# Regrouping score rows by two ten-row transfers with spaced source rows, in a talking-heads attention and gated layer kernel

## The chip, the cores and the metric

The kernel runs on one core of one Trainium2 chip, in one launch. The metric is the device time of that launch in microseconds (us). Times are compared by medians of several runs; the trace that is read here is of one profiled execution. Engines are named as the profile names them: PE (TensorE matmul), PEld (its weight load), DVE (VectorE), ACT (ScalarE), POOL (GpSimd), SP (SyncE, which issues transfers here).

## What is computed

Batch 4, 12 heads, 448 positions, head dimension 64, all in float32. Cut to what matters:

```python
scores = scale * np.matmul(q, k.transpose(0, 1, 3, 2))
scores = np.einsum('bhij,hg->bgij', scores, w_pre)      # first mix over heads
scores = scores - np.max(scores, axis=-1, keepdims=True)
attn = np.exp(scores)
attn = attn / (np.sum(attn, axis=-1, keepdims=True) + 1e-09)
attn = np.einsum('bhij,hg->bgij', attn, w_post)         # second mix over heads
attn_out = np.matmul(attn, v)
x = attn_out.transpose(0, 2, 1, 3).reshape(1792, 768)
gate = 1.0 / (1.0 + np.exp(-(x @ w_gate)))              # 768 x 1536
val = x @ w_val
return gate * val @ w_out                               # 1536 x 768
```

The two mixes contract over heads, so a query row of all 12 heads has to lie on the partitions before it can be mixed by a matmul.

## The kernel before

The attention is cut into 16 blocks: four per batch, of 120, 120, 120 and 88 query rows. Scores of a block are made on PE, two heads at a time (`scores`, L134), and copied to an SBUF tile `st` with query rows on the partitions and, in each partition, 12 heads by 448 keys (`keep`, L143; even pairs of heads on DVE, odd ones on ACT). There are two such tiles, one for even and one for odd blocks.

A block is then worked off in sets of ten rows; two sets make a unit, so a block of 120 rows has six units and one of 88 rows has nine sets (the last begins at row 78 and repeats two rows) and so five units, the last with one set. In all there are 92 units: 88 with two sets and 4 with one. For each unit:

- `regroup` (L169) moves score rows from `st` into a tile `T`, of which there are three. Each transfer takes five neighbouring partitions of `st` (five query rows) and writes 60 partitions of `T` (row by head), 448 floats each. A unit with two sets needs four transfers, all issued by SP: the first set lies on partitions 0 to 59, the second on 64 to 123, and the two halves of a set lie beside each other in the free dimension (index x).
- `premix` (L178) is the first mix: four PE matmuls of 60 rows by 448 columns against the block diagonal weights `w1`, into PSUM banks `pm`. `rowmax` (L186, DVE), `expo` (L194, ACT), `norm` (L202, DVE), `scale` (L207, POOL) and `p_lo` (L223, DVE) make the softmax, split in two float16 parts for most units (`pairs`); the first 6 and the last 8 units stay in float32 and scale the weights instead.
- `postmix` (L231) is the second mix, which also brings keys onto the partitions; `mix` (L243, ACT) copies it from its one PSUM tile into the tile `mixes` of the block. `av` (L251) multiplies by v, copies the result (ACT) and stores it to DRAM from ACT's queue.

The order of work is written out by hand, slot by slot (L345 to L391), one slot per unit. In slot s the program issues, in this order: `regroup(s + 4)`; `premix(s + 2)` and `rowmax(s + 2)`; the scores of the next block that are due; `norm` and `scale` of unit s + 1; `mix(s - 1)`; the copies of those scores; `p_lo(s + 1)`; loads of q, k and v from ACT's queue; `expo(s + 2)`; tasks of the gated layer; `postmix(s)`; and the `av` steps that are due. Every engine runs its own instructions in this order. `regroup(u)` can start when its `T` is free, that is when `premix(u - 3)` is done, and when its block's `st` is complete; the copy of a later block into the same `st` has to wait for the last regroup of the block before the last. The transfers of SP and of ACT take turns on a few completion semaphores, so a transfer is issued only when the one that had its semaphore before has landed.

The gated layer (class `_Moe`, from L414) is a planned list of tasks: its weights are loaded, converted and split in the last units of the attention and behind it, and its matmuls (L818 and L829) fill PE to the end.

Of the kernel before, what the change touches and what calls it, by code (L numbers as in the profile page):

```python
# [22 lines left out]
R = 10  # L23
HALF = 5
# [3 lines left out]

def _blocks(S):
    return [(i0, min(QB, S - i0)) for i0 in range(0, S, QB)]  # L30


def _key_blocks(S):
    return [0, 128, 256, S - 128]


def _attention(ctx, tc, ins, B, H, S, D, xs, raws, make_moe):

    nc = tc.nc
    qp, kp, vb = (ins[n] for n in ("qp", "kp", "vb"))  # L40
# [3 lines left out]
    HK = HALF * H  # L44
# [3 lines left out]
    JB = _key_blocks(S)  # L48
# [18 lines left out]
    PM = 3  # L67
    pm = ps_pm.tile([128, PM, 512], F32, name="pm")

    def two_banks(pool, tag):  # L70
        return pool.tile([128, 2, 512], F32, tag=tag, name=tag)
# [3 lines left out]
    w1 = const.tile([128, 64], F32, name="w1")  # L75
# [24 lines left out]
    blocks, units, NG, ring = [], [], 0, 0  # L100
    for b in range(B):
        for i0, n in _blocks(S):
            rows = [min(r0, n - R) for r0 in range(0, n, R)]
            blocks.append((b, i0, n, len(units)))
            for i in range(0, len(rows), 2):
                r0s = rows[i:i + 2]
                units.append((len(blocks) - 1, r0s, [(ring + k) % PM for k in range(len(r0s))], NG))
                ring += len(r0s)
                NG += len(r0s)
    NU = len(units)  # L110
# [12 lines left out]

    def q_load(bi, eng=None):

        b, i0, n, _ = blocks[bi]
        t = qst.tile([128, NP * QB], F32, tag="q", name="q")
        (eng or nc.scalar).dma_start(out=t[:, :NP * n], in_=qp[b, :, NP * i0:NP * (i0 + n)])
        q_t[bi] = t[:, :NP * n].rearrange("p (c s) -> p c s", s=n)


    st_t = {}

    def scores(bi, c, sc):  # L134
        b, _, n, _ = blocks[bi]
        q, k = q_t[bi], k_t[b, c]
        cuts = [(0, 64), (64, n)] if n > 96 else [(0, n)]
        for s0, s1 in cuts:
            for e in range(2):
                rows = slice(64 * e, 64 * e + 64)  # L140
                nc.tensor.matmul(sc[s0:s1, e, :S], lhsT=q[rows, c, s0:s1], rhs=k[rows, :], start=True, stop=True)  # L141

    def keep(bi, c, sc):  # L143
        n = blocks[bi][2]
        if c == 0:
            st_t[bi] = stg[bi % 2].tile([QB, H, S], F32, tag="st", name="st")
        out, src = st_t[bi][:n, 2 * c:2 * c + 2], sc[:n, :, :S]
        if c % 2:
            nc.scalar.copy(out, src)
        else:  # L150
            nc.vector.tensor_copy(out, src)  # L151
# [10 lines left out]
    t_t, nm_t, e_t, ss_t, p_t, mx_t = {}, {}, {}, {}, {}, {}  # L162
    mixes = [mp.tile([128, 4, H, QB], F32, name=f"mix{i}") for i in range(2)]

    def pairs(u):

        return PB + 2 <= u < NU - 8

    def regroup(u):  # L169
        bi, r0s, _, _ = units[u]  # L170
        T = tp.tile([128, 2, S], F32, tag="T", name="T")
        for i, r0 in enumerate(r0s):
            for x in range(2):
                r = r0 + HALF * x
                nc.sync.dma_start(out=T[64 * i:64 * i + HK, x], in_=st_t[bi][r:r + HALF])  # L175
        t_t[u] = T

    def premix(u):  # L178
# [52 lines left out]
    def postmix(u):  # L231
        m = len(units[u][1]) * R
        mx = two_banks(ps_mx, "mx").rearrange("p b (h c) -> p (b h) c", h=2)[:, :, :H * m]
        mx = mx.rearrange("p j (g r) -> p j g r", r=m)
        for i, (a, b) in enumerate(p_t.pop(u)):
            terms = [(a, w2hi), (a, w2lo), (b, w2hi)] if pairs(u) else [(a, b)]
            for jb in range(4):
                for k, (lhs, w) in enumerate(terms):
                    nc.tensor.matmul(mx[:, jb, :, R * i:R * i + R], lhsT=lhs[:, JB[jb]:JB[jb] + 128], rhs=w,  # L239
                                     start=(k == 0), stop=(k == len(terms) - 1))  # L240
        mx_t[u] = mx

    def mix(u):  # L243
        bi, r0s, _, _ = units[u]
        nc.scalar.activation(out=mixes[bi % 2][:, :, :, r0s[0]:r0s[-1] + R], in_=mx_t.pop(u), func=AF.Copy,  # L245
                             scale=1.0 / (P_UP * W_UP))

# [1 line left out]
    av_t = {}  # L249

    def av(bi, c):  # L251
        b, i0, n, _ = blocks[bi]
        u, h = divmod(2 * c, QUAD)
        if c % 4 == 0:
            last = bi == NBK - 1 and c
            t = two_banks(ps_mx, "mx")[:, 0] if last else ps_av.tile([128, 512], F32, tag="av", name="av")
            av_t[bi] = t[:, :4 * QB].rearrange("p (c s) -> p c s", c=4)
        for jb in range(4):
            for i in range(2):
                nc.tensor.matmul(av_t[bi][64 * i:64 * i + 64, c % 4, :n], lhsT=vt[b, u][:, h + i, jb, :],  # L260
                                 rhs=mixes[bi % 2][:, jb, 2 * c + i, :n], start=(jb == 0), stop=(jb == 3))
        if c % 4 == 3 or c == KC - 1:
            c0 = c - c % 4
            if bi == NBK - 1:
                xt = mixes[1 - bi % 2][:, c // 4, :4][:, :c + 1 - c0, :n]
            else:
                xt = xp.tile([128, 4, QB], F32, tag="xt", name="xt")[:, :c + 1 - c0, :n]
            nc.scalar.activation(out=xt, in_=av_t.pop(bi)[:, :c + 1 - c0, :n], func=AF.Copy, scale=sw)
            nc.scalar.dma_start(out=xs[b, c0:c + 1, :, i0:i0 + n].rearrange("c p s -> p c s"), in_=xt)
# [18 lines left out]
    for bi in range(1, NBK):  # L288
        s0, s1 = first[bi - 1] - LEAD, first[bi] - LEAD
        for c in range(NP):  # L290
            at(spread(c, NP, s0, s1), scores, bi, c)
        if bi > 1:
            at(s0 - 4, q_load, bi)
# [24 lines left out]

    k_load(0, 0, nc.sync)
    q_load(0, nc.sync)  # L320
    for c in range(1, NP):
        k_load(0, c, nc.sync)
# [75 lines left out]
def _weight_order(FN):  # L398

    quarters = ((0, 0), (0, 1), (1, 0), (1, 1))  # L400
    order = [(n,) + q for n in range(FN) for q in quarters]
    order += [(FN + j,) + q for q in quarters[:2] for j in range(OUT_TILES)]
    return order + [(FN + j,) + q for j in range(OUT_TILES) for q in quarters[2:]]
# [470 lines left out]
@with_exitstack  # L874
def kernel(ctx, tc, B, H, S, D, ins, out):
    nc = tc.nc
    top = ctx.enter_context(tc.tile_pool(name="top", bufs=1))
    dram = ctx.enter_context(tc.tile_pool(name="dram", bufs=1, space=DRAM))
    xs = dram.tile([B, H * D // 128, 128, S], F32, name="xs")
    with tc.manual_schedule():  # L880
        raws = top.tile([128, 13 * H * D // 2], F32, name="raws")
        with ExitStack() as c2:
            moe = _attention(c2, tc, ins, B, H, S, D, xs, raws,
                             lambda NG: _Moe(tc, xs, ins, out, raws, NG))
        moe.run()


def _laid_out(q, k, v, w_pre, w_post, moe_w_gate, moe_w_val, moe_w_out):

    B, H, S, D = q.shape  # L890
    NQ, NP = H // QUAD, H // 2
    a = {}

    qt = q.reshape(B, NP, 2, S, D).transpose(0, 2, 4, 1, 3).reshape(B, 2 * D, NP, S)
    a["qp"] = np.concatenate([qt[..., i0:i0 + n].reshape(B, 2 * D, -1) for i0, n in _blocks(S)], axis=2)
    a["kp"] = k.reshape(B, NP, 2, S, D).transpose(0, 1, 2, 4, 3).reshape(B, NP, 2 * D, S)

    vb = np.stack([v[:, :, j:j + 128] for j in _key_blocks(S)], axis=3)
    vb[:, :, :4 * 128 - S, 3] = 0
    a["vb"] = vb.reshape(B, NQ, QUAD, 128, 4, D).transpose(0, 1, 3, 2, 4, 5).reshape(B, NQ, 128, -1)  # L900

    w1 = np.zeros((128, 64), w_pre.dtype)
    w2 = np.zeros((128, H, R), w_post.dtype)
    for x in range(2):
        for r in range(HALF):
            at = slice(64 * x + r * H, 64 * x + (r + 1) * H)
            w1[at, r * H:(r + 1) * H] = w_pre
            w2[at, :, HALF * x + r] = w_post
    a["w1"] = w1
    a["w2"] = w2.reshape(128, H * R)  # L910
    a["wpc"] = np.broadcast_to(w_post.reshape(-1), (128, H * H))


    KH, FH = moe_w_gate.shape[0] // 2, moe_w_gate.shape[1] // 2
    gv = np.stack([w.reshape(2, KH // 128, 128, 2, FH // 128, 128) for w in (moe_w_gate, moe_w_val)])
    gv = gv.transpose(5, 4, 1, 3, 0, 2, 6)
    o = moe_w_out.reshape(2, OUT_TILES, FH // 128 // OUT_TILES, 128, 2, KH).transpose(1, 4, 0, 3, 2, 5)
    tiles = [(gv[n] if n < len(gv) else o[n - len(gv)])[i, j] for n, i, j in _weight_order(FH // 128)]
    a["w"] = np.stack([t.reshape(128, -1) for t in tiles])
    return a  # L920
# [36 lines left out]
```

## Time and profile before

| | us |
|---|---|
| median of 3 runs | 1165.29 |
| lowest and highest | 1158.84 and 1168.05 |
| the profiled execution, its own time | 1167.52 |
| its span, first to last instruction | 1165.7 |

The profile's page gives for each engine the busy time and its share of the span. The chain of work that ended last is followed back from the last instruction, at each step to what released it; "T<-st" in it is a transfer of `regroup` under way, "SPq L175" is SP's queue spending time on issuing one. A window's row gives busy time by engine, the granted share of PE's full clock, the mean busy share of the core's 16 DMA engines, and the rate at which they moved data. A line "x8" in a timeline or in a chain stands for eight instructions merged.

### The profile page before, as it was taken

To read this page: it belongs to the slowest core of one execution; us is meant where nothing else is said; L and a number is where in the kernel's file an instruction comes from. 1 tells how busy PE (TensorE), PEld (TensorE's weight loads), DVE (VectorE), ACT (ScalarE), POOL (GpSimd) and SP (SyncE) were. 2 spreads that over 40 slices of the span, in tenths; PEclk is the share of its full clock that TensorE was granted. 3 is DMA by queue.
4 is the path that set the end of the run, shared out by engine and by line. 5 is a ranking of instruction groups with operands and counts; after the bars stand their busy time and mean duration, and the time that the engine had idled before them with its cause. 6 is when DMAs were issued, how large, how long until landed. Compare 5 with 4: busy or idle time off the path is not lost.

```text
span 1165.7 us, 18485 instructions
## 1 busy us (share of the span) xinstructions
PE 975.0 (84%) x7262; PEld 724.1 (62%) x7262; DVE 685.1 (59%) x959; ACT 546.5 (47%) x919; POOL 120.0 (10%) x192
## 2 busy tenths in 40 slices
PE   6867588776788675887758799999989999999998
PEld 1333354343444343544434588999968999999997
DVE  2235454444554444544434568888899886658992
ACT  2333353343443343533444557766865554445541
POOL 0011121111111111111113400000000000000000
PEclk8888799978897887988879889999988999999999
DMA  3244333343333443333533625655886241220001
GB/s 122 63 112 127 84 86 82 92 129 107 83 82 78 111 128 88 84 86 93 147 116 110 207 64 205 232 189 187 284 296 214 75 155 59 79 69 16 13 11 71
DMA packets 68910, 135.21 MB, mean 116 GB/s; under 512 B 18296, under 2 KB 49240, under 8 KB 68824
## 3 DMA queue, kind: packets, MB, share of 16 engines
q1 hardware_dynamic: 47768, 106.91, 30.1%
q10 hardware_dynamic: 20288, 24.38, 7.3%
q0 software_dynamic: 768, 2.75, 0.7%
q8 instruction: 57, 0.93, 0.3%
q14 instruction: 29, 0.24, 0.1%
HBM read 70.15 MB, written 25.17 MB: 82 GB/s over the span
## 4 chain that ended last, share of the span: by engine, by line
PE 57%; DMA 21%; SPq 13%; ACT 3%; DVE 3%; issue 2%; ACTq 1%; POOL 0%; DVEq 0%; POOLq 0%
PE bank L818 26%; DMA T<-st 19%; SPq L175 13%; PE bank L829 12%; PE mx L239 6%; PE pm L184 5%; PE av L260 4%; PE qk L141 3%; DMA k<-in_kp_dram 2%; ACT e L198 1%; ACT mix L245 1%; DVE st L151 1%; DMA raws<-in_w_dram 1%; DVE m_GV L808 1%; DVE m_FWTR L811 1%
## 5 line engine op out<-in xcount | busy, mean ns | idle before, releaser
L818 PE MATMUL bank<-m_GV 128*128 128x448 f32 x1512 | 310.4, 367 | 1.3 <-DVE m_GV L808 0.7
L818 PEld LDWEIGHTS bank<-m_GV 128*128 128x128 f32 x1512 | 283.9, 188 | 27.3 <-DVE m_GV L808 1.1
L191 DVE TENSOR_REDUCE nm<-pm 128x2 f32<-128x896 f32 (+1 forms) x92 | 98.5, 1071 | 279.6 <-PE pm L184 278.2
L184 PE MATMUL pm<-T,w 60*64 60x448 f32 x720 | 155.5, 627 | 78.8 <-ACT e L198 48.7
L198 ACT ACTIVATE e<-pm,nm 128x448 f32<-128x448 f32 x180 | 112.8, 634 | 178.5 <-DVE ss L204 70.4
L808 DVE TENSOR_TENSOR m_GV<-m_FWTR,m_GV 128x768 fp32r<-128x768 f32 (+1 forms) x139 | 156.1, 1135 | 56.0 <-ACT m_GV L805 55.7
L239 PEld LDWEIGHTS <-ph 128*128 128x128 f16 x1224 | 102.2, 107 | 130.2 <-issue 125.9
L239 PE MATMUL mx<-w2hi,ph 128*128 128x120 f16 x612 | 118.0, 234 | 65.9 <-ACT mix L245 65.9
L829 PE MATMUL bank<-m_GV 128*128 128x448 f32 x756 | 161.2, 375 | 8.5 <-ACT m_GV L805 7.3
L805 ACT CAST m_GV<-m_FWTR 128x768 fp32r<-128x768 f32 (+1 forms) x139 | 134.2, 980 | 65.2 <-DVE m_FWTR L811 24.3
L829 PEld LDWEIGHTS bank<-m_GV 128*128 128x128 f32 x756 | 145.5, 193 | 23.8 <-ACT m_GV L805 8.0
L141 PE MATMUL qk<-k,q 64*56 64x448 f32 (+2 forms) x640 | 130.1, 638 | 21.8 <-DVE st L151 21.2
L215 POOL TENSOR_SCALAR ph<-e,ss 128x448 f16<-128x448 f32 x153 | 95.7, 638 | 456.2 <-DVE ss L205 423.2
L227 DVE SCALAR_TENSOR_TENSOR pl<-e,ss,ph 128x448 f16<-128x448 f32 x153 | 120.7, 827 | 35.5 <-POOL ph L215 35.5
L245 ACT ACTIVATE mix<-mx 128x960 f32<-128x960 f32 (+1 forms) x92 | 87.8, 954 | 107.4 <-DMA T<-st 94.5
L239 PE MATMUL mx<-w2hi,pl 128*128 128x120 f16 x612 | 118.4, 235 | 0.0
L184 PEld LDWEIGHTS pm<-T,w 60*64 60x64 f32 x720 | 33.1, 144 | 137.3 <-DMA T<-st 69.6
L239 PE MATMUL mx<-w2lo,ph 128*128 128x120 f16 x612 | 118.2, 235 | 0.0
L260 PE MATMUL av<-mix,v 128*64 128x120 f32 (+1 forms) x1504 | 104.8, 291 | 0.0
L260 PEld LDWEIGHTS av<-mix,v 128*64 128x64 f32 x1504 | 84.6, 154 | 10.5 <-PE mx L239 2.7
L835 ACT COPY m_FWTR<-bank 128x448 f32<-128x448 f32 x96 | 51.2, 533 | 80.8 <-PE bank L818 58.7
L141 PEld LDWEIGHTS qk<-k,q 64*64 64x64 f32 (+2 forms) x640 | 34.4, 149 | 81.2 <-issue 42.0
(58 smaller groups left out, 731.4 us busy)
## 6 DMA issues: line engine op xcount, KB each, us to landing
T<-st SPq DMA_DIRECT2D x360, 105.0 KB
raws<-in_w_dram SPq DMA_DIRECT2D x32, 767.6 KB
w<-m_FWTR SPq DMA_DIRECT2D x36, 384.0 KB
m_FWTR<-w SPq DMA_DIRECT2D x30, 384.0 KB
raws<-w SPq DMA_DIRECT2D x18, 384.0 KB
v<-in_vb_dram ACTq DMA_DIRECT2D x12, 512.0 KB
out_dram<-m_FWTR SPq DMA_DIRECT2D x24, 224.0 KB
k<-in_kp_dram ACTq DMA_DIRECT2D x18, 224.0 KB
```

The source lines that it names most:

```text
L141: nc.tensor.matmul(sc[s0:s1, e, :S], lhsT=q[rows, c, s0:s1], rhs=k[rows, :], start=True, stop=True)
L175: nc.sync.dma_start(out=T[64 * i:64 * i + HK, x], in_=st_t[bi][r:r + HALF])
L184: nc.tensor.matmul(pm[64 * x:64 * x + 64, bank, :S], lhsT=w1[rows], rhs=T[rows, x], start=True, stop=True)
L198: nc.scalar.activation(out=e[:, i], in_=pm[:, bank, :S], func=AF.Exp, bias=nm, scale=1.0, accum_out=ss[:, i:i + 1])
L227: nc.vector.scalar_tensor_tensor(pl[:, i], e_t[u][:, i], ss_t[u][:, i:i + 1], ph, op0=ALU.mult, op1=ALU.subtract)
L239: nc.tensor.matmul(mx[:, jb, :, R * i:R * i + R], lhsT=lhs[:, JB[jb]:JB[jb] + 128], rhs=w, start=(k == 0), stop=(k == len(terms) - 1))
L245: nc.scalar.activation(out=mixes[bi % 2][:, :, :, r0s[0]:r0s[-1] + R], in_=mx_t.pop(u), func=AF.Copy, scale=1.0 / (P_UP * W_UP))
L260: nc.tensor.matmul(av_t[bi][64 * i:64 * i + 64, c % 4, :n], lhsT=vt[b, u][:, h + i, jb, :], rhs=mixes[bi % 2][:, jb, 2 * c + i, :n], start ...
L805: self.nc.scalar.copy(self.f32(hi).bitcast(F32R), self.f32(f))
L808: self.nc.vector.tensor_tensor(self.f32(lo).bitcast(F32R), self.f32(f), self.f32(hi), op=ALU.subtract)
L818: self.nc.tensor.matmul(self.f32(bank), lhsT=w[a][:, k], rhs=x[b][:, k], start=self.START[i] and k == r == 0, stop=k == self.KH - 1 and r ...
L829: self.nc.tensor.matmul(self.f32(bank), lhsT=w[a][:, k], rhs=b[bb], start=self.START[i] and j == k == r == 0, stop=j == OUT_TILES - 1 and ...
```

## The change

`regroup` now moves all ten rows of one set in one transfer. For this the rows of a block lie in another order on the partitions of `st`: the host lays q out so that row r of set j is at partition r * sets + j (sets is 12 or 9), with the two repeated rows stored twice, so a block of 88 rows has 90 partitions. A transfer reads ten partitions that are 12 (or 9) apart and writes 120 neighbouring partitions of `T`. Index x of `T` is now the set, and the partitions are the ten rows. The second half of a set then begins at partition 60 and not 64. `premix` still reads partitions 64 to 123, so a second transfer per set copies the first four heads of row five to partitions 120 to 123, and the second half of `w1` is turned by four rows to fit. A unit with one set has two transfers of five rows, as before. `premix` is unchanged in its instructions; since x and the half have changed places in its output, `postmix` writes its result in runs of five columns instead of ten.

```diff
+def _sets(n):
+    return [min(r0, n - R) for r0 in range(0, n, R)]
...
     def regroup(u):
-        bi, r0s, _, _ = units[u]
+        bi, r0s, _, _, i = units[u]
+        sets, st = blocks[bi][4], st_t[bi]
         T = tp.tile([128, 2, S], F32, tag="T", name="T")
-        for i, r0 in enumerate(r0s):
+        for x in range(2):
+            if len(r0s) == 2:
+                nc.sync.dma_start(out=T[:2 * HK, x], in_=st[i + x:sets * R:sets])
+            else:
+                nc.sync.dma_start(out=T[:HK, x], in_=st[i + sets * HALF * x:sets * HALF * (x + 1):sets])
+        if len(r0s) == 2:
+            p = i + sets * HALF
             for x in range(2):
-                r = r0 + HALF * x
-                nc.sync.dma_start(out=T[64 * i:64 * i + HK, x], in_=st_t[bi][r:r + HALF])
+                nc.sync.dma_start(out=T[2 * HK:64 + HK, x], in_=st[p + x:p + x + 1, :64 - HK])
         t_t[u] = T
...
     def postmix(u):
         m = len(units[u][1]) * R
         mx = two_banks(ps_mx, "mx").rearrange("p b (h c) -> p (b h) c", h=2)[:, :, :H * m]
-        mx = mx.rearrange("p j (g r) -> p j g r", r=m)
+        mx = mx.rearrange("p j (g x r) -> p j g x r", g=H, x=2)
...
-                    nc.tensor.matmul(mx[:, jb, :, R * i:R * i + R], lhsT=lhs[:, JB[jb]:JB[jb] + 128], rhs=w,
+                    nc.tensor.matmul(mx[:, jb, :, :, HALF * i:HALF * i + HALF], lhsT=lhs[:, JB[jb]:JB[jb] + 128],
+                                     rhs=w.rearrange("p g (x r) -> p g x r", x=2),
                                      start=(k == 0), stop=(k == len(terms) - 1))
...
-    a["qp"] = np.concatenate([qt[..., i0:i0 + n].reshape(B, 2 * D, -1) for i0, n in _blocks(S)], axis=2)
+    rows = [i0 + np.add.outer(np.arange(R), _sets(n)).reshape(-1) for i0, n in _blocks(S)]
+    a["qp"] = np.concatenate([qt[..., r].reshape(B, 2 * D, -1) for r in rows], axis=2)
...
-            w1[at, r * H:(r + 1) * H] = w_pre
+            w1[(60 * x + r * H + np.arange(H) - 64) % 60 + 64 if x else at, r * H:(r + 1) * H] = w_pre
```

`scores`, `keep` and `q_load` take the number of rows as ten times the number of sets (120 or 90) instead of 120 or 88; `mix` and `av` are as before.

## Rows read from the trace of the kernel before

**Rows 1.** The page's chain that ended last: shares by engine, and by line.

```profile
PE 57%; DMA 21%; SPq 13%; ACT 3%; DVE 3%; issue 2%; ACTq 1%; POOL 0%; DVEq 0%; POOLq 0%
PE bank L818 26%; DMA T<-st 19%; SPq L175 13%; PE bank L829 12%; PE mx L239 6%; PE pm L184 5%; PE av L260 4%; PE qk L141 3%; DMA k<-in_kp_dram 2%; ACT e L198 1%; ACT mix L245 1%; DVE st L151 1%; DMA raws<-in_w_dram 1%; DVE m_GV L808 1%; DVE m_FWTR L811 1%
```

**Rows 2.** Instructions of L175, L191, L818: count, ns min/median/max, first and last start.

```profile
L175 SPq DMA_DIRECT2D T<-st x360: 742/1642/3552, 12.8 to 647.5; - x180
L191 DVE TENSOR_REDUCE nm<-pm x92: 617/1092/1093, 25.9 to 662.5; 128x2 f32<-128x896 f32 x88, 128x1 f32<-128x448 f32 x4
L818 PE MATMUL bank<-m_GV x1512: 362/367/742, 677.4 to 1084.4; 128*128 128x448 f32 x189
```

**Rows 3.** Tile T: who waited for its transfers (us, times).

```profile
  ACT mix L245: 94.5, 24
  PEld pm L184: 69.6, 57
  DVE st L151: 30.1, 9
  PE pm L184: 29.7, 31
  ACT e L198: 22.9, 6
  ACT st L149: 13.9, 2
  ACT xt L268: 12.7, 3
```

**Rows 4.** The chain in order of time, 310 to 318 us: start, us, what.

```profile
310.28 0.91 PE pm L184 x8
311.20 0.75 PE qk L141 x8
311.95 1.37 PE mx L239 x24
313.32 0.97 PE av L260 x16
314.29 0.91 PE pm L184 x8
```

**Rows 5.** SP's timeline around 300 us: start, us, line, transfers issued.

```profile
288.32 59.27 SPq L175 DMA_DIRECT2D T<-st  x33
...
319.28 2.01 SPq L175 DMA_DIRECT2D T<-st  x1
...
325.88 0.74 SPq L175 DMA_DIRECT2D T<-st  x1
```

**Rows 6.** Windows: engines busy, clock, DMA share, GB/s.

```profile
300.00:360.00 60.00, 48.89 (x508) 28.41 (x512) 28.55 (x49) 25.09 (x51) 10.64 (x17) 0.87 0.33 84
640.00:680.00 40.00, 30.62 (x248) 24.65 (x249) 14.90 (x23) 21.92 (x36) 12.63 (x13) 0.77 0.59 193
740.00:860.00 120.00, 120.00 (x584) 109.10 (x583) 102.36 (x140) 90.22 (x123) 0.00 (x0) 1.00 0.66 228
308.00:320.00 12.00, 11.96 (x152) 7.64 (x150) 7.40 (x12) 6.83 (x15) 2.50 (x4) 0.92 0.36 90
```

**Rows 7.** Transfer issues: size of T<-st; ns of a 384 KB store, of av's stores.

```profile
T<-st SPq DMA_DIRECT2D x360, 105.0 KB
L791 SPq DMA_DIRECT2D w<-m_FWTR x36: 319/320/526, 649.1 to 867.9; - x36
L269 ACTq DMA_DIRECT2D xs<-xt x30: 366/383/389, 120.6 to 678.1; - x30
```

**Rows 8.** Timelines and chain: the first unit, a transfer, one block turn, one ACT wait.

```profile
18.41 0.96 PE L184 MATMUL pm<-T,w 60*64 60x448 f32 x2 [2.42 <-DMA T<-st]
25.94 1.09 DVE L191 TENSOR_REDUCE nm<-pm 128x2 f32<-128x896 f32 x1 [10.98 <-PE pm L184]
297.48 5.63 DMA T<-st
316.02 0.91 ACT L149 COPY st<-qk 120x896 f32<-120x896 f32 x1 [1.22 <-PE qk L141]
281.67 0.97 ACT L245 ACTIVATE mix<-mx 128x960 f32<-128x960 f32 x1 [6.92 <-DMA T<-st]
304.48 1.76 PE qk L141 x4
666.86 2.02 PE mx L239 x16
```

More of the change, by code (lines that the diff above doesn't have):

```diff
@@ L102, in _attention @@
         for i0, n in _blocks(S):
-            rows = [min(r0, n - R) for r0 in range(0, n, R)]
-            blocks.append((b, i0, n, len(units)))
+            rows = _sets(n)
+            blocks.append((b, i0, n, len(units), len(rows)))
             for i in range(0, len(rows), 2):
                 r0s = rows[i:i + 2]
-                units.append((len(blocks) - 1, r0s, [(ring + k) % PM for k in range(len(r0s))], NG))
+                units.append((len(blocks) - 1, r0s, [(ring + k) % PM for k in range(len(r0s))], NG, i))
                 ring += len(r0s)
@@ L124, in q_load @@
     def q_load(bi, eng=None):
-        b, i0, n, _ = blocks[bi]
+        b, i0, _, _, sets = blocks[bi]
+        n = R * sets
         t = qst.tile([128, NP * QB], F32, tag="q", name="q")
@@ L134, in scores @@
     def scores(bi, c, sc):
-        b, _, n, _ = blocks[bi]
+        b, n = blocks[bi][0], R * blocks[bi][4]
         q, k = q_t[bi], k_t[b, c]
@@ L143, in keep @@
     def keep(bi, c, sc):
-        n = blocks[bi][2]
+        n = R * blocks[bi][4]
         if c == 0:
@@ L238, in postmix @@
                 for k, (lhs, w) in enumerate(terms):
-                    nc.tensor.matmul(mx[:, jb, :, R * i:R * i + R], lhsT=lhs[:, JB[jb]:JB[jb] + 128], rhs=w,
+                    nc.tensor.matmul(mx[:, jb, :, :, HALF * i:HALF * i + HALF], lhsT=lhs[:, JB[jb]:JB[jb] + 128],
+                                     rhs=w.rearrange("p g (x r) -> p g x r", x=2),
                                      start=(k == 0), stop=(k == len(terms) - 1))
-        mx_t[u] = mx
+        mx_t[u] = mx.rearrange("p j g x r -> p j g (x r)")
     def mix(u):
-        bi, r0s, _, _ = units[u]
+        bi, r0s = units[u][:2]
         nc.scalar.activation(out=mixes[bi % 2][:, :, :, r0s[0]:r0s[-1] + R], in_=mx_t.pop(u), func=AF.Copy,
@@ L251, in av @@
     def av(bi, c):
-        b, i0, n, _ = blocks[bi]
+        b, i0, n = blocks[bi][:3]
         u, h = divmod(2 * c, QUAD)
```

## The prediction

> **What bounds the kernel now.** I read the page's chain first, because it says what the end of the run waited for [rows 1]. Half of it is the gated layer's matmuls (L818, L829). The striking part is T<-st with 19% and SP's issuing of it (L175) with 13%: together 32% of 1165.7 us, about 373 us, in which PE is not what the run waits for.
>
> Next come the instruction rows, which date the stages [rows 2]. The first `rowmax` starts at 25.9 us and the last of 92 at 662.5, so a unit takes (662.5 - 25.9) / 91 = 7.00 us. The gated layer's matmuls begin at 677.4 and have 488 us to the end. The 360 regroup issues span 12.8 to 647.5 us at a median of 1.642 us: 360 x 1.642 = 591 us of some 636, and four of them, one unit, are 6.57 us. SP is thus issuing nearly all the time; its timeline shows 33 issues in 59.27 us with no pause [rows 5].
>
> Is that the price of issuing, or does SP stand behind full DMA queues? The floor of an issue is 0.742 us [rows 2], and it recurs beside one of 2.01 us of the same shape [rows 5]. Stores of 384 KB from 128 partitions are issued in 0.32 us [rows 7]. So most of the 1.64 us is pushback. The windows say from where [rows 6]: in 300 to 360 us the DMA share is 0.33, which is 5.3 of 16 engines, at 84 GB/s, or 15.9 GB/s per busy engine; in 740 to 860 us it is 0.66 at 228 GB/s, or 21.6 per busy engine. A regroup looks like work for about five engines, at a poor pace. At 105.0 KB [rows 7], or 107.5 kB, a transfer is 21.5 kB for each of five; four are 86 kB, and 86 / 15.9 = 5.4 us of each unit, before the other loads.
>
> Finally, what would a unit cost if its T were there? The chain from 310 to 314 us has one such slot, and PE fills it: premix 0.91, scores 0.75, second mix 1.37, av 0.97, together 4.00 us, and the next premix starts 4.01 after this one [rows 4]. In 308 to 320 us PE is busy 11.96 of 12 us, DVE 7.40, ACT 6.83, POOL 2.50 [rows 6]: PE is next in line.
>
> **The change part by part.**
>
> *The ten-row transfers.* Still four issues per two-set unit and 360 in all (88 x 4 + 4 x 2), but two are of 215 kB and two of 7.2 kB (four rows of 1792 bytes). If ten rows go to ten engines, each engine gets 2 x 21.5 = 43 kB per unit, some 2.0 us at the pace of 740 to 860 us and 2.7 at that of 300 to 360 [rows 6]; if still five, 86 kB, 4.0 to 5.4 us. I take ten, because the load seen matches one engine per source row. [...]
>
> *Issuing.* No row shows a 120-row issue. Lower bound for each of the four 0.32 us [rows 7]; upper bound for a large one twice the floor, 1.48, and for a small one 0.74 [rows 2]: 1.28 to 4.45 us per unit. I take 1.1 for the large, midway between one floor and two, and 0.38, an ACT store's price [rows 7], for the small: 3.0 us. That is below PE's 4.0, so SP stops being the conveyor.
>
> *Latency.* A transfer took 5.63 us from the start of its issue to landing in a crowd [rows 8]; so T(u) is there at most 2.6 + 5.6 = 8.2 us after SP starts it. It may start when premix(u - 3) is over and is wanted three slots later, 12.0 - 0.9 = 11.1 us. At a block turn the last copy ends at 316.02 + 0.91 = 316.93 and the premix that needs it is due three slots after 314.29, at 326.3: 9.4 us. Both hold, the second barely, so turns may cost a little.
>
> *Second mix and `w1`.* Premix has the same four matmuls, at nothing extra. The second mix keeps its 24 matmuls of 120 columns, in runs of five; from no cost to twice 1.37 us. With runs of ten a matmul takes 1.37 / 24 = 57 ns for 120 columns [rows 4], with no sign of a price per run; I take nothing. Two more score rows in a 90-row block: nothing, PE streams the 448 keys.
>
> *The sum.* PE's work: per batch 23 x (0.91 + 1.37) + 24 x (0.75 + 0.97) = 93.7 us, four times 375. The 14 float32 units have a second mix of 2.02 instead of 1.37 [rows 4, 8]: + 9. The first block's scores are made ahead: 6 x 0.75, - 5. Total 379. It starts at about 20 us: SP begins at 12.8 [rows 2] and T(0) lands up to 8.2 later (the first premix now begins at 18.41 but its `rowmax` at 25.94 [rows 8]).
> What stays of the waits: ACT stood 94.5 + 22.9 + 13.9 + 12.7 = 144 us for T [rows 3], mostly behind its own store or load, which waits for the semaphore a transfer still holds (6.92 us in one case [rows 8]). With transfers landing early most of it goes; I keep a sixth, 24 us, bounds 0 and half, 72. From the last `rowmax` to 677.4 are 14.9 us, of which two slots of 2.02 + 0.97 are in the 379: 9 stay. Gated layer from 20 + 379 + 24 + 9 = 432 us instead of 677.4, 245 us earlier. Its 488 us I leave: its preparation fits in the shorter slots, since in 640 to 680 us DVE is busy 14.9 and ACT 21.9 of 40 us [rows 6], though not by much; up to 10 us may be lost there.
> Span 1165.7 - 245.4 = 920; the profiled execution's own time is 1.8 over its span, so 922, and the median of the runs is 2.2 under that execution: about **921**. Nothing of the waits left gives 921 - 24 - 9 = 888; half of them 969.
>
> **The rivals.**
>
> *Residual waits.* SP at its upper price, 4.45 us per unit, becomes the bound: 92 x 4.45 = 409, 30 us more, 951; with half of ACT's waits as well, 999. For: 0.742 may be the price of 60 rows. Against: 128 rows go out in 0.32.
>
> *PE runs slow.* The clock was 0.87 in 300 to 360 us and 1.00 in the dense 740 to 860 [rows 6]; after a wait the scores took 1.76 and not 0.75 [rows 4, 8]. If it stays at 0.87, 379 becomes 436: 978. I count this with the one before, since it needs the waits.
>
> *Still five engines.* 5.4 us per unit: 497 instead of 379 + 24, 1015.
>
> *Short runs cost PE.* 78 float16 units by 1.37: + 107, 1028.
>
> *Nothing changes.* The time could belong to the transfer and not to its bytes: four are still four, 6.57 us per unit, 1165. [...] Against the mechanism stands the floor of 0.742 for the same shape and 0.32 for a transfer more than three times as large.
>
> *Slower.* If 1.64 us is SP's own price for 60 rows, a large transfer costs 3.28 and a small one still 0.74: 8.04 against 6.57, + 1.47 x 92 = 135, 1300. It decides from a large issue of (6.57 - 1.48) / 2 = 2.5 us. The same two rows speak against it.
>
> **How the numbers follow.** The forecast (888 to 969) 0.68; residual waits or a slow clock (to 1000) 0.15; five engines 0.08; short runs 0.02; nothing changes 0.03; slower 0.04. A measurement here tells about 1% from no change. Faster 0.68 + 0.15 + 0.08 + 0.02 = 0.93, same 0.03, slower 0.04. The range takes the first two cases, 888 to 1000, and leaves out 0.17.
>
> **What would show it.** Right: `rowmax` every 4.1 to 4.5 us; L818 from about 432; large issues of 0.7 to 1.5 us with pauses between; waits for T down to a few tens of us; PE nearly full at a clock near 1.00 in the attention; the stretch behind L818's start still 488 us. Wrong: large issues over 2 us (SP the conveyor still); a DMA share of 0.33 with `rowmax` every 5 us or more (five engines); second mix above 1.37 in a warm slot (short runs); a gated layer that takes over 500 us, with PE waiting for weights.

## The result, and the profile after

| | us |
|---|---|
| before, median of 4 runs beside it | 1166.17 |
| after, median of 4 runs (946.34 to 948.80) | 947.42 |
| ratio, with its 95% interval | 0.813 (0.809 to 0.816) |
| after: span of the profiled execution | 944.5 |

The change makes the kernel about 19% faster, 219 us. The forecast was 921 us, 26 less than measured, in a range of 888 to 1000.

The page's chain after, by engine and by line; compare [rows 1]:

```profile
PE 79%; ACT 7%; DVE 4%; DMA 4%; issue 2%; ACTq 1%; SPq 1%; POOL 0%; DVEq 0%
PE bank L831 33%; PE bank L842 14%; PE mx L251 14%; PE av L273 8%; PE pm L196 6%; PE qk L147 5%; ACT mix L258 3%; ACT e L210 2%; ACT xt L281 2%; DMA T<-st 1%; DMA raws<-in_w_dram 1%; ACTq L282 1%; DVE m_GV L821 1%; DVE nm L203 1%; DMA k<-in_kp_dram 1%
```

T<-st has fallen from 19% to 1%, and SP's part from 13% to 1%. PE has 79% instead of 57%. As PE takes over the chain, the shares of all its steps in the attention go up. The second mix (PE mx) goes up most: it is 14% of 944.5 us, 132, where it was 6% of 1165.7, some 70; av goes from some 47 to 76.

The instruction rows after: ten-row transfers (L181), the four-row pieces (L187), the lone sets (L183), `rowmax` (L203) and the gated layer's matmul (L831), with ns min/median/max and first and last start; compare [rows 2]:

```profile
L181 SPq DMA_DIRECT2D T<-st x176: 788/810/1086, 12.4 to 418.6; - x176
L187 SPq DMA_DIRECT2D T<-st x176: 611/642/1407, 14.2 to 420.1; - x176
L183 SPq DMA_DIRECT2D T<-st x8: 777/780/798, 104.6 to 422.4; - x8
...
L203 DVE TENSOR_REDUCE nm<-pm x92: 624/1092/1093, 17.9 to 440.5; 128x2 f32<-128x896 f32 x88, 128x1 f32<-128x448 f32 x4
...
L831 PE MATMUL bank<-m_GV x1512: 361/368/472, 454.6 to 863.1; 128*128 128x448 f32 x189
```

An issue of 120 rows takes 0.81 us, hardly more than the old floor of 0.742 for 60, and it hardly varies: the pushback is gone. A unit now takes (440.5 - 17.9) / 91 = 4.64 us instead of 7.00, and the gated layer starts at 454.6 instead of 677.4.

Who waited for T after (us, times), without `rowmax`, whose wait is for premix and not for a transfer; compare [rows 3]:

```profile
  ACT st L155: 4.5, 3
  PEld pm L196: 2.6, 4
  DVE st L157: 2.0, 7
  PE pm L196: 1.9, 1
```

11.0 us are left of the 273.4 of [rows 3]. The windows after (PE, PEld, DVE, ACT, POOL busy, then clock, DMA share, GB/s); compare [rows 6]:

```profile
200.00:260.00 60.00, 58.07 (x758) 38.70 (x760) 43.02 (x72) 36.39 (x76) 15.65 (x25) 1.00 0.38 132
300.00:360.00 60.00, 56.46 (x726) 37.02 (x723) 42.08 (x71) 34.76 (x71) 14.59 (x24) 1.00 0.34 120
...
455.00:860.00 405.00, 393.75 (x1970) 357.35 (x1969) 324.22 (x401) 242.25 (x334) 0.00 (x0) 0.99 0.44 149
```

PE is nearly full in the attention, 58.07 and 56.46 of 60 us, at a granted clock of 1.00. And the DMA engines move 132 GB/s at a share of 0.38: 21.7 GB/s per busy engine instead of 15.9, the pace that the window of large loads showed before the change, 21.6.

The chain of one stretch after (start, us, what), first a slot in which PE waits for nothing, then one with an av copy; compare [rows 4]:

```profile
214.78 0.91 PE pm L196 x8
215.69 0.75 PE qk L147 x8
216.45 1.74 PE mx L251 x24
218.19 0.99 PE av L273 x16
219.18 0.02 issue
219.20 0.47 ACT xt L281
219.67 0.02 issue
219.69 0.38 ACTq L282
220.08 0.05 issue
220.12 0.98 ACT mix L258
221.10 0.04 issue
221.14 1.79 PE mx L251 x24
```

Premix, scores and av cost what they did. The second mix has gone from 1.37 to 1.74 us: that is where most of the forecast's missing 26 us lie, and the experiments go after it.

### The profile page after: what moved, and what is told of

Read it like the earlier page. It is cut to its first block, busy times and chain, and to the rows that moved or that the text cites. A ratio compares the mean times of both kernels' runs of the same rounds, so it can differ in the third digit from the quotient of the medians.

```text
span 944.5 us, 18487 instructions
## 1 busy us (share of the span) xinstructions
PE 895.9 (95%) x7262; PEld 703.2 (74%) x7262; DVE 685.2 (73%) x959; ACT 545.8 (58%) x919; POOL 119.5 (13%) x192
## 4 chain that ended last, share of the span: by engine, by line
PE 79%; ACT 7%; DVE 4%; DMA 4%; issue 2%; ACTq 1%; SPq 1%; POOL 0%; DVEq 0%
PE bank L831 33%; PE bank L842 14%; PE mx L251 14%; PE av L273 8%; PE pm L196 6%; PE qk L147 5%; ACT mix L258 3%; ACT e L210 2%; ACT xt L281 2%; DMA T<-st 1%; DMA raws<-in_w_dram 1%; ACTq L282 1%; DVE m_GV L821 1%; DVE nm L203 1%; DMA k<-in_kp_dram 1%
## 5 line engine op out<-in xcount | busy, mean ns | idle before, releaser
L831 PE MATMUL bank<-m_GV 128*128 128x448 f32 x1512 | 312.3, 368 | 1.3 <-DVE m_GV L821 0.7
L831 PEld LDWEIGHTS bank<-m_GV 128*128 128x128 f32 x1512 | 283.5, 188 | 29.4 <-DVE m_GV L821 1.1
L818 ACT CAST m_GV<-m_FWTR 128x768 fp32r<-128x768 f32 (+1 forms) x139 | 134.1, 979 | 68.0 <-DVE m_FWTR L824 25.1
L203 DVE TENSOR_REDUCE nm<-pm 128x2 f32<-128x896 f32 (+1 forms) x92 | 98.6, 1071 | 95.9 <-PE pm L196 90.9
L251 PEld LDWEIGHTS <-ph 128*128 128x128 f16 x1224 | 104.9, 107 | 65.5 <-issue 65.0
L251 PE MATMUL mx<-w2hi,ph 128*128 128x120 f16 x612 | 126.2, 242 | 11.3 <-ACT mix L258 11.3
L251 PE MATMUL mx<-w2hi,pl 128*128 128x120 f16 x612 | 127.7, 243 | 0.0
L251 PE MATMUL mx<-w2lo,ph 128*128 128x120 f16 x612 | 127.0, 243 | 0.0
L196 PE MATMUL pm<-T,w 60*64 60x448 f32 x720 | 94.2, 567 | 6.3 <-ACT e L210 4.2
L147 PE MATMUL qk<-k,q 64*64 64x448 f32 (+2 forms) x640 | 93.3, 552 | 6.2 <-DVE st L157 6.0
L273 PE MATMUL av<-mix,v 128*64 128x120 f32 (+1 forms) x1504 | 93.5, 270 | 0.0
L273 PEld LDWEIGHTS av<-mix,v 128*64 128x64 f32 x1504 | 74.8, 139 | 11.9 <-issue 0.4
L851 DVE TENSOR_TENSOR m_FWTR<-bank,m_FWTR 128x448 f32<-128x448 f32 x90 | 55.9, 622 | 36.1 <-PE bank L842 20.7
L824 DVE TENSOR_TENSOR m_FWTR<-m_FWTR 128x768 f32<-128x768 f32 (+1 forms) x67 | 77.5, 1167 | 0.2 <-DMA m_FWTR<-w 0.2
```

What stands on the lines that cost most here:

```text
L196: nc.tensor.matmul(pm[64 * x:64 * x + 64, bank, :S], lhsT=w1[rows], rhs=T[rows, x], start=True, stop=True)
L203: nc.vector.tensor_reduce(nm[:, :len(banks)], src, axis=AX.X, op=ALU.max, negate=True)
L251: nc.tensor.matmul(mx[:, jb, :, :, HALF * i:HALF * i + HALF], lhsT=lhs[:, JB[jb]:JB[jb] + 128], rhs=w.rearrange("p g (x r) -> p g x r", x= ...
L818: self.nc.scalar.copy(self.f32(hi).bitcast(F32R), self.f32(f))
L831: self.nc.tensor.matmul(self.f32(bank), lhsT=w[a][:, k], rhs=x[b][:, k], start=self.START[i] and k == r == 0, stop=k == self.KH - 1 and r ...
```

## Experiments

Medians are of four runs, and ratios are against runs of the kernel before on the same chip, where that was measured between 1165.6 and 1166.4 us; runs_of_four and runs_of_three ran once each.

### The second mix alone put right: ten_runs

In the changed kernel a PSUM bank of a unit holds half of each of two sets, which is why the second mix has to write runs of five. Which ten query rows these are is only a matter of the order in which the host lays out q:

```diff
+def _row_order(n):
+    sets = _sets(n)
+    order = np.add.outer(np.arange(R), sets)
+    for s in range(0, len(sets) - 1, 2):
+        for x in range(2):
+            for i in range(2):
+                order[HALF * i:HALF * i + HALF, s + x] = sets[s] + R * i + HALF * x + np.arange(HALF)
+    return order.reshape(-1)
...
-                    nc.tensor.matmul(mx[:, jb, :, :, HALF * i:HALF * i + HALF], lhsT=lhs[:, JB[jb]:JB[jb] + 128],
-                                     rhs=w.rearrange("p g (x r) -> p g x r", x=2),
+                    nc.tensor.matmul(mx[:, jb, :, R * i:R * i + R], lhsT=lhs[:, JB[jb]:JB[jb] + 128], rhs=w,
```

> The changed kernel with another order of rows on the host: each unit's twenty rows are placed so that the second mix writes its 120 columns in runs of ten again, with the transfers as in the changed kernel. In the changed kernel the 24 float16 matmuls of a slot take 1.74 us from the first to the start of av, before the change 1.37. Theory A, that the runs of five cost this: back to 1.37, 78 units x 0.37 = 29 us less than the changed kernel's 947, so 918, and a slot of 4.0 us. Rival B, that the second mix is slower since the transfers or the other engines are now denser beside it: the matmuls stay at 1.74 and the time within 5 us of 947.

Measured: 923.9 us, ratio 0.790 (0.785 to 0.796), against 0.813 (0.809 to 0.816) of the changed kernel. Its chain in about the same stretch:

```profile
202.82 0.91 PE pm L207 x8
203.73 0.75 PE qk L158 x8
204.48 1.37 PE mx L262 x24
205.85 0.99 PE av L283 x16
```

The second mix is back at 1.37 us with the same transfers beside it, and the time falls by 23.5 us of the 29 expected. Theory A holds: the runs of five cost it, not the traffic around. The matmuls as built differ in the output's pattern alone, since the weights, which are contiguous, are read in one run either way. This kernel is faster than the changed one.

### Spread without merging, merging without spread: spaced_five and ten_adjacent

The change does two things to a transfer. spaced_five takes the kernel before, its four five-row transfers and its second mix, and only lays the rows 12 (or 9) partitions apart:

```diff
-                r = r0 + HALF * x
-                nc.sync.dma_start(out=T[64 * i:64 * i + HK, x], in_=st_t[bi][r:r + HALF])
+                r = i + j + sets * HALF * x
+                nc.sync.dma_start(out=T[64 * j:64 * j + HK, x], in_=st[r:sets * HALF * (x + 1):sets])
```

> The kernel before with one thing changed: the rows of a block are spread over the partitions of st as in the changed kernel, so each of its four five-row transfers per unit reads partitions 12 (or 9) apart instead of neighbours. Four transfers of 107.5 kB, second mix in runs of ten, w1 as before. Theory S, that neighbouring source rows held the engines back: a transfer on five engines at 21.6 GB/s per engine is 1.0 us, a unit 4.0 us, about PE's slot; issues at 0.75 to 1.0 us each; 915 to 960 us. Rival E, that the number of engines was the bound: still 86 kB for each of five at the old pace, issues near 1.6 us, and no gain, 1130 to 1170 us.

ten_adjacent takes the changed kernel, runs of five included, with ten neighbouring source rows:

```diff
-                nc.sync.dma_start(out=T[:2 * HK, x], in_=st[i + x:sets * R:sets])
+                nc.sync.dma_start(out=T[:2 * HK, x], in_=st[r0s[x]:r0s[x] + R])
```

> The changed kernel with the other half of the change alone: ten-row transfers and everything else as there, second mix in runs of five too, but rows in natural order on the partitions, so a transfer reads ten neighbouring partitions. Theory S (neighbouring source rows): the ten engines are held back as the five were; SP's issues rise well over the 0.81 us of the changed kernel, a unit costs 5.5 to 7 us, 1040 to 1170 us. Rival E (number of engines): as the changed kernel, 947 us within 10.

Measured: spaced_five 966.8 us, 7 above the range expected, ratio 0.828 (0.823 to 0.833); ten_adjacent 1146.2, ratio 0.983 (0.975 to 0.990). The issues of spaced_five, and of ten_adjacent (ten rows, then four):

```profile
L182 SPq DMA_DIRECT2D T<-st x360: 742/742/1101, 13.1 to 441.3; - x180
```

```profile
L180 SPq DMA_DIRECT2D T<-st x176: 788/814/2646, 12.4 to 621.6; - x176
L186 SPq DMA_DIRECT2D T<-st x176: 642/2506/3263, 14.3 to 625.0; - x176
```

With spread rows the median issue of a five-row transfer is its floor, 0.742 us, where it was 1.642. With ten neighbours SP is pushed back as before, only that the wait now shows at the small transfer behind the large ones: 2 x 0.81 + 2 x 2.51 = 6.6 us per unit, the old 6.57. Theory S holds. The spacing is worth about 200 us by itself (1166 to 967), the merging 20 (1166 to 1146, with the costlier second mix). On top of the spacing, merging gives another 43 (967 to 924, both with runs of ten). They lie in the attention: from 15 us to the first matmul of the gated layer (at 473.9 in spaced_five, at 426.7 in ten_runs) PE stands for 61 us in spaced_five and for 35 in ten_runs, and it is busy for 398 us instead of 377, at a granted clock of 0.95 instead of 1.00. Part of the standing is seen in spaced_five's waits:

```profile
PE mx L246 <- ACT mix L252: 35.5, 30, 4.0
...
ACT mix L252 <- DMA T<-st: 23.6, 10, 4.1
```

Transfers still land late enough there that ACT stands for a semaphore, 23.6 us in ten cases, and the second mix waits for ACT's copy for 35.5 us, where it is 16.6 in ten_runs. Neither ten_runs nor the changed kernel has an entry of mix behind a transfer.

### How far apart is apart: step_four and step_two

spaced_five again, with the five source rows of a transfer four or two partitions apart (STEP).

```diff
+STEP = 4
+def _place(j, r):
+    return HALF * STEP * (j // STEP) + j % STEP + STEP * r
...
+                p = _place(2 * (i + j) + x, 0)
+                nc.sync.dma_start(out=T[64 * j:64 * j + HK, x], in_=st[p:p + STEP * (HALF - 1) + 1:STEP])
```

> The kernel spaced_five (966.8 us) with the five source rows of a transfer four partitions apart instead of twelve; the last block has 100 partitions instead of 90, with ten rows that nobody reads. Theory G, that partitions of one aligned group of four share something that engines read through, and that rows of different groups don't disturb each other: as spaced_five, 967 us within 12, issues at a median of 0.74 us. Rival D, that distance counts gradually: clearly slower than spaced_five, 1000 us or more. [...]

> The same with the five source rows two partitions apart, so that a group of four partitions holds two of them. Theory G: two engines share, which lies between one (967 us) and three or four (1166 us): 980 to 1080 us, issues at a median between 0.8 and 1.5 us. Rival N, that only directly neighbouring partitions disturb each other: 967 us within 12.

Measured: step_four 964.9 us, ratio 0.827 (0.821 to 0.832); step_two 1061.2, ratio 0.909 (0.904 to 0.914). Issues of step_four, then of step_two, and after them one window of each in the same order:

```profile
L206 SPq DMA_DIRECT2D T<-st x360: 742/745/1279, 12.5 to 436.4; - x180
```

```profile
L206 SPq DMA_DIRECT2D T<-st x360: 742/1378/2742, 12.4 to 532.4; - x180
```

```profile
300.00:360.00 60.00, 56.13 (x749) 36.32 (x748) 41.62 (x69) 36.51 (x76) 14.76 (x24) 0.96 0.37 124
```

```profile
300.00:360.00 60.00, 47.99 (x552) 27.48 (x544) 34.03 (x56) 27.74 (x58) 12.51 (x20) 0.91 0.45 135
```

Four apart is as good as twelve; two apart lies about half way. Rivals D and N both fall. By pace per busy engine, over all traffic of the window: 124 / (0.37 x 16) = 20.9 GB/s with a step of four, 135 / (0.45 x 16) = 18.8 with two, 15.9 with one [rows 6]. So neighbours disturb each other here and rows four apart don't, as theory G has it. What neighbouring rows share is not seen in the trace, and that the group of four is aligned was not tested by itself.

The packets of SP's queue, which has the regroup alone between 200 and 330 us, show the holding back itself. The lines are of the kernel before, step_two, step_four, ten_adjacent and the changed kernel in this order (packets, MB, share of the time of 16 engines):

```profile
q1 hardware_dynamic: 4693, 7.76, 23.8%
```

```profile
q1 hardware_dynamic: 5770, 9.55, 24.9%
```

```profile
q1 hardware_dynamic: 6998, 11.57, 24.6%
```

```profile
q1 hardware_dynamic: 5356, 8.63, 39.3%
```

```profile
q1 hardware_dynamic: 7405, 11.96, 24.9%
```

From MB and share over these 130 us come 15.7 GB/s per busy engine for five neighbours, 18.4 two apart, 22.6 four apart, 10.6 for ten neighbours and 23.1 for ten rows apart. Packet by packet, five or fewer of this queue are under way at once for 97% of these 130 us in the kernel before, and ten or fewer for 90% in the changed kernel. With ten neighbours 39.3% of 16, 6.3 engines, are busy with them on average, with five 3.8. So merging did bring more engines, as the prediction had it, but among neighbouring rows each of them became slower, 10.6 GB/s instead of 15.7.

### Is it the reading or the writing: read_five

In ten_runs the weights get a gap after every five columns, so that the matmul reads runs of five and writes runs of ten.

```diff
-    w2hi = const.tile([128, H, R], F16, name="w2hi")
+    w2hi = const.tile([128, H, 2, HALF + 1], F16, name="w2hi")[:, :, :, :HALF]
```

> The kernel ten_runs with the float16 weights of the second mix held with a gap after every five columns, so that the matmul's moving operand is read in runs of five while the result is written in runs of ten. If the writing of short runs costs: second mix 1.37 us, as ten_runs, about 918 us. If the reading of short runs costs (the float32 units, with 20 bytes in a run of five where float16 has 10, show no loss in the changed kernel): 1.74 us and about 947 us.

Measured: 937.1 us, ratio 0.802 (0.797 to 0.806). Neither figure expected came out. The second mix in its chain:

```profile
201.53 1.61 PE mx L265 x24
```

1.61 us: reading a gapped operand costs 0.24 us of its own. It doesn't explain the changed kernel, which reads without gaps; there the writing alone costs 0.37.

### A price per run, or a threshold: full_run, runs_of_four, runs_of_three

full_run writes all 120 columns of a matmul in one run, at the price of a copy in two ACT instructions:

```diff
-        mx = mx.rearrange("p j (g r) -> p j g r", r=m)
+        mx = mx.rearrange("p j (i g r) -> p j i g r", g=H, r=R)
...
+                    nc.tensor.matmul(mx[:, jb, i], lhsT=lhs[:, JB[jb]:JB[jb] + 128], rhs=w,
```

> The kernel ten_runs with the second mix writing its 120 columns in one run; the copy that follows (mix) is made of two ACT instructions instead of one, 0.58 us each instead of 0.97 in all. If each run costs PE time (24 runs 1.74 us, 12 runs 1.37), a single run is cheaper still: 1.22 to 1.30 us, 5 to 12 us less for PE, of which ACT's 0.19 us more per unit takes a part back: 910 to 925 us. If runs of ten are already free and only runs of five cost: the 24 matmuls stay at 1.37 and the time is 924 to 940.

runs_of_four and runs_of_three write the columns in 30 and 40 short runs (q is 4 and 3):

```diff
+                        flat = mx.rearrange("p j g r -> p j (g r)").rearrange("p j (c e q) -> p j c e q", e=2, q=4)
+                        out, w = flat[:, jb, :, i], w.rearrange("p g r -> p (g r)").rearrange("p (c q) -> p c q", q=4) if len(w.shape) == 3 and w.shape[2] == R else w
```

> The kernel ten_runs with one thing changed: the float16 second mixes of two-set units write their 120 columns in 30 runs of four instead of 12 of ten. The columns then stand in another order than the next step takes them, so the result is not the reference's; the work is the same. Measured is the step from the first of the 24 matmuls to the start of av: 1.37 us with 12 runs of ten and with one run of 120, 1.74 with 24 runs of five. Theory P, that what costs is a broken pair of columns: an even run is free, 1.37 us. [...] Rival R, that short runs cost by their number: 30 runs cost more than 24, 1.8 us or more.

> The same with 40 runs of three; the columns are out of order in the same way, so the result is not the reference's. Theory P: 80 pairs are touched where runs of five touch 72 and even runs 60, so a good deal over 1.74 us, about 1.9. Rival R: 40 runs, 2.0 us or more; with runs_of_four at 1.37 it has fallen whatever this gives.

Measured: full_run 932.6 us, ratio 0.799 (0.795 to 0.802); runs_of_four 920.9 and runs_of_three 948.9 in one run each. full_run came out as expected for the case that runs of ten are already free. The second mix in the chains of the three, in this order:

```profile
200.48 1.37 PE mx L262 x24
```

```profile
204.20 1.37 PE mx L266 x24
```

```profile
204.70 1.79 PE mx L266 x24
```

One run of 120, 12 of ten and 30 of four all take 1.37 us; 24 of five take 1.74 and 40 of three 1.79. The granted clock is 1.00 between 200 and 230 us in all of them, and 0.980, 0.987 and 0.986 over the whole of the three runs. The number of runs is thus not what costs, and rival R falls: the runs that cost here are the odd ones, of five and of three. This fits theory P, though no view shows pairs of columns. My size for runs of three, 1.9, was too high.

The starts of the 24 matmuls say more (medians over the 75 float16 units with two sets). In ten_runs and runs_of_four they follow each other at 52 to 53 ns. In the changed kernel the twelve of the first set, whose runs of five begin at even columns, follow at 63, and those of the second set, whose runs begin at odd columns, at 72 to 73. In runs_of_three it is 70 in both sets. An odd run thus costs also where it begins at an even column. Why the odd start costs more with runs of five, and not with runs of three, is open.

full_run's split copy, 0.58 us twice instead of 0.97, costs 9 us in all and gives PE nothing.

### What is left of the waits: late_copy and full_late

In ten_runs ACT's copy of av's result and its store are moved behind the next mix.

```diff
+            def finish():
+                nc.scalar.activation(out=xt, in_=src, func=AF.Copy, scale=sw)
+                nc.scalar.dma_start(out=xs[b, c0:c + 1, :, i0:i0 + n].rearrange("c p s -> p c s"), in_=xt)
+            if s < NU:
+                late.append(finish)
...
         for args in kept:
             keep(*args)
+        while late:
+            late.pop(0)()
```

> The kernel ten_runs (923.9 us) with one step of ACT moved: the copy of av's result and its store, which stood ahead of the next unit's mix on ACT, are issued behind that mix. In ten_runs the chain in a slot with such a copy goes av, copy 0.47 to 0.67 us, store issue 0.38, mix 0.97, and the second mix of the next unit waits for it. Theory A, that the waits that are left in the attention are this order and not the transfers: some 28 slots gain 0.3 to 0.9 us, 898 to 916 us. Rival B, that ACT is simply full or the transfers are late again: within 5 us of 924.

> late_copy and full_run together. If both gains are PE's and independent: their sum, 890 to 910 us. If ACT, which then has both the split copies and the later copy, becomes the bound: not below late_copy.

Measured: late_copy 938.1 us, ratio 0.803 (0.800 to 0.807), 14 more than ten_runs; full_late 937.6, ratio 0.804 (0.800 to 0.807), no faster than late_copy. late_copy fits neither theory: it is slower. Some waits in ten_runs, then in late_copy (us, times, longest):

```profile
ACT st L166 <- PE qk L158: 45.1, 24, 3.8
...
PE mx L262 <- ACT mix L268: 16.6, 30, 2.4
...
PE pm L207 <- ACT e L221: 6.8, 10, 2.3
```

```profile
ACT st L166 <- PE qk L158: 59.5, 43, 3.6
...
PE pm L207 <- ACT e L221: 27.8, 28, 2.2
...
PE mx L262 <- ACT mix L268: 7.3, 7, 2.8
```

The second mix waits less for ACT, 7.3 us instead of 16.6. But `expo` empties the PSUM banks that the next premix needs, and premix waits for it 27.8 us instead of 6.8. `expo` has the same work ahead of it on ACT in both kernels. In ten_runs av's copy and its store run before ACT has to wait for the scores; in late_copy they stand behind that wait, which grew from 45.1 to 59.5 us, and so `expo` comes later. The wait moved from one PE step to another and grew; that the order on ACT does it is read from these rows and was not tested by itself. In full_late the split copy, which cost full_run 9 us, changes nothing on top of that.

## Why the prediction was right, and where it was off

- **Bound.** Right. SP's issuing was pushback, the transfers were the conveyor, and PE was next in line: it is nearly full in the attention, and the gated layer starts at 454.6 instead of 677.4.
- **Ten-row transfers.** Right in size: the pace is 21.7 GB/s per busy engine, the better of the two forecast. But the text weighed the number of engines and treated the poor pace as a bound; it never named the neighbouring source rows as its cause. spaced_five shows that five-row transfers do nearly as well once the rows lie apart (967 us), and ten_adjacent that merging alone hardly helps (1146). Here the forecast had luck: its reasoning would have been the same for ten neighbouring rows, and it was right because the change happened to spread them too. The rival of still five engines was priced at 1015; with five-row transfers from spread rows, and with runs of ten, it measured 967.
- **Issuing.** 2 x 0.81 + 2 x 0.64 = 2.9 us per unit against 3.0 taken; the large issue was dearer in the forecast (1.1), the small one cheaper (0.38).
- **Second mix.** This step failed. The sum took nothing for runs of five, from rows that showed only runs of ten, and gave the short runs a chance of 0.02 at a doubling. They cost 0.37 us in each of 75 units, 28 us (three of the 78 float16 units have one set and still write one run). The bounds held the value; the choice inside them didn't. A second mix above 1.37 us in a slot without waits was the sign that the text had named for this rival, and a unit every 4.64 us lies outside its 4.1 to 4.5.
- **The sum otherwise.** First premix about 15 instead of 20, since the first issues were not pushed back (four in 3.2 us, where seven took 11.5 before): -5. Work 379 + 28 = 407, where PE is busy for 408 between 15 and 454.6 us; the 379 counts the four units with one set as whole ones, some 5 us too many, so the other steps took a little more. The other 31 or 32 us are waits and tail, against 24 + 9. The gated layer takes 944.5 - 454.6 = 489.9 us instead of 488. Together -5 + 28 - 1 + 2 = 24 of the 26. The text's last step has a slip of 1 us: 920.3 + 1.8 - 2.2 is 920 and not 921. With the one term mended in the kernel, ten_runs measures 923.9.

```profile
15.00:454.60 439.60, 408.44 (x4828) 267.92 (x4820) 296.31 (x488) 265.68 (x540) 119.31 (x188) 0.98 0.48 161
```

- **What the 24 us of waits are.** Right in amount, wrong in kind. They were put down to ACT waiting for transfers; ACT's waits for them have gone from 144 us to 4.5. About half of what is left is ACT's own order, as in the chain above: av, copy, store, mix, then the second mix 0.3 us late. The rest is DVE's copies of scores, `expo` (4.2 us), a stretch with no releaser in the profile ("issue") and 1.9 us for T. late_copy shows that ACT's order can't simply be turned.

```profile
PE mx L251 <- ACT mix L258: 15.4, 29, 2.5
...
PE qk L147 <- DVE st L157: 6.0, 4, 1.6
...
PE mx L251 <- issue: 4.6, 3, 2.2
```

- **Nothing changes.** This rival gave the time to the transfer and not to its bytes, with four transfers per unit before and after. Four now take 2.9 us of issuing instead of 6.57, and a unit comes every 4.64 us instead of 7.00.

## What to carry to other kernels

When issues on a queue are slow and irregular beside a floor that recurs, look behind the queue; here the median was 1.64 us beside a floor of 0.742. The neighbourhood of the partitions that a transfer reads set its pace here, 15.7 GB/s per busy engine with five neighbours and 22.6 with five rows four apart. Their number mattered less: ten instead of five was worth 20 us among neighbours and 43 with the rows apart, the spacing about 200. A layout that spreads them may cost nothing, as here where only the host's order of rows changes; four and twelve apart did equally well, 964.9 and 966.8 us, and other distances than two, four and twelve (nine in the last block of a batch) were not tried. When a change turns a matmul's output pattern, don't take it as free: here runs of three and five cost, 1.79 and 1.74 us for 24 matmuls, runs of four, ten and 120 didn't, 1.37, and another order of rows on the host gave the runs of ten back. A term that no row shows should not be put at the end of its bounds that one prefers.

## What the runs showed of the hardware that was not expected

- Transfers that read five neighbouring partitions were issued at a median of 1.64 us, two apart at 1.38, four apart at 0.745, twelve apart at 0.742.
- A float16 matmul of 120 columns cost 1.37 / 24 = 57 ns with output runs of 4, 10 or 120 float32 values, 72 ns with 5, 75 with 3 (the step through all 24, up to the start of av); reading its moving operand in runs of five float16 values with a gap cost 67. The float32 second mix took 2.02 us in runs of ten [rows 8] and was not slowed in the changed kernel:

```profile
435.69 2.02 PE mx L251 x16
```

- Twice the rows in a transfer cost 0.81 against 0.742 us of issuing, and a transfer of only four rows still 0.64.
